# Chunked attention and a gated channel mix: scores in 64-row array tiles, softmax by units of 256 tokens, the gate in single PSUM banks

## The chip, the cores and the metric

The kernel runs on one core of a Trainium2 chip. The time is the device time of one execution in microseconds, as the median of several runs. The engines are named as in the profile: PE multiplies matrices (PEld is its weight loads), DVE works on vectors, ACT on scalar functions, POOL is the general engine, SP issues the transfers.

## What is computed

Four sequences of 768 tokens, 8 heads of 64. Attention is local: chunks of 32 queries see 16 tokens to the left, their own 32, 8 to the right, and 8 memory keys, 64 keys in all. The output, 512 wide, goes through a gated channel mix with a token shift.

```python
for c in range(S // 32):
    l_start, r_end = max(0, 32 * c - 16), min(S, 32 * c + 32 + 8)
    k_full = np.concatenate([mem_k, k[:, :, l_start:r_end]], axis=2)
    v_full = np.concatenate([mem_v, v[:, :, l_start:r_end]], axis=2)
    scores = scale * np.matmul(q_c, k_full.transpose(0, 1, 3, 2))
    a = np.exp(scores - scores.max(-1, keepdims=True))
    out[:, :, 32 * c : 32 * c + 32] = np.matmul(a / (a.sum(-1, keepdims=True) + 1e-9), v_full)
# x: out as (4, 768, 512)
xk = mu_k * x + (1 - mu_k) * x_prev          # x_prev: the token before
xr = mu_r * x + (1 - mu_r) * x_prev
k = np.maximum(xk @ w_k, 0)                  # 512 x 1024
v = k * k @ w_v                              # 1024 x 512
return 1 / (1 + np.exp(-(xr @ w_r))) * v     # 512 x 512
```

## The kernel before

Tokens come in query tiles of 128 (24 of them, four chunks of 32 each) and in units of 256, two tiles (12 units). Everything is float32. The three weight products of the channel mix are each done as three products of rounded parts (`fp32r`, high and low halves; `wkh` and `wkl` are the halves of `w_k`, `xh` and `xl` those of the mixed input).

For a tile, `attention` has these steps, named as the profile and the plan name them:

- **s**: 16 matmuls, one for each pair of heads and each chunk. The two heads of a pair lie in the two halves of the 128 rows. The host lays the queries out block-diagonally, with zeros for the other head, so that the 64 result columns are 32 queries of one head and 32 of the other. A matmul takes 128 rows and 64 columns, an even chunk writes partitions 0 to 63 and an odd one 64 to 127 of one PSUM bank (`s4[o : o + 64, ...]`).
- softmax on 512 columns: maximum (`mx`), subtraction (`e`), exponential, sum, normalisation on DVE or POOL.
- **t** (`pt`): four transposes; copies into `aTz`, whose other half is zero.
- **a** (`px`): 16 matmuls with `vw`, 64 columns each; a copy (`f_x`) turns the result into `xT`.

`prep` makes the mixed inputs of a unit (`df`, `xf`, then `xh` and `xl`, for the gate first). In `channel_mix`, **g** (`pr`) is the gate, 24 matmuls into a tile of two PSUM banks, which one sigmoid reads; **h** (`ph`) is the product with `w_k`, four groups of 24; **v** (`pv`) the product with `w_v`, 24 for each tile of the unit, planned in halves.

The order is set by a planner inside the kernel. `te_order` writes out a sequence for PE, beginning with `LEAD`, and derives due times from it with `PE_COST`; every step has an engine or a choice, a cost, and buffers (`Slot`, counted in `bufs`). `Plan.order` places steps greedily, and the result is issued in that order on every engine. Where the plan leaves PE idle before the first `ph`, the kernel issues matmuls on zeros (`warm`), their number worked out from the planned gap:

```python
n = 0 if ("ph", 0, 0) in T else int((o.start - busy - 0.2) / (0.22 if busy else 0.43))
```

[...] The buffers `big` hold query and key tiles (`qk`) and raw weights in turn.

Of the kernel before, what the change touches and what calls it, by code (L numbers as in the profile page):

```python
# [16 lines left out]
P = 128  # L17
# [23 lines left out]
PE_COST = {"s": 1.05, "t": 0.45, "a": 1.05, "g": BLOCK, "h": BLOCK, "v": BLOCK}  # L41
# [94 lines left out]
def te_order():  # L136

    nu = B * S // UTOK
    seq = LEAD.split()
    seq = [tuple([x[0]] + [int(n) for n in x[1:].split(".")]) for x in seq]  # L140
    for u in range(nu):
        a, b = 2 * u + 4, 2 * u + 5
        g = [("g", u + 1, c) for c in range(QPU)] if u + 1 < nu else []
        h = [("h", u, f) for f in range(FT // 2)]
        v = [("v", u, c, n) for c in range(QPU) for n in range(2)]
        seq += h[:2] + [("t", a)] + h[2:3] + [("a", a), ("s", b)] + h[3:] + g + [("t", b)]
        seq += v[:1] + [("a", b), ("s", a + 2)] + v[1:]
    nq = B * NQT
    seq = [x for x in seq if not (x[0] in "sta" and x[1] >= nq)]
# [9 lines left out]
def local_attention__then__channel_mix(  # L159
# [126 lines left out]
    xslot = {}  # L286

    def attention(t):
        b, i = qts[t]
        u, c = t // QPU, t % QPU  # L290

        def f_load():
            a = T["qk", t] = sb("big", [P, QKW], f"qk{t}")
            nc.sync.dma_start(a, qk[b, i])
# [5 lines left out]
        def f_s():  # L300
            s = T["s", t] = ps("s", f"s{t}")
            s4 = s.rearrange("p (m r k) -> p m r k", m=2, r=NPAIR)
            a = T["qk", t]
            nq = NPAIR * NJ * 2 * CHUNK
            q4 = a[:, :nq].rearrange("p (r j q) -> p r j q", r=NPAIR, j=NJ)
            k4 = a[:, nq:].rearrange("p (r j k) -> p r j k", r=NPAIR, j=NJ)
            for r in range(NPAIR):
                for j in range(NJ):
                    o = 64 * (j % 2)
                    nc.tensor.matmul(  # L310
                        s4[o : o + 64, j // 2, r, :], q4[:, r, j, :], k4[:, r, j, :], start=True, stop=True
                    )

        def f_max():
            s = T["s", t].rearrange("p (m r k) -> p m r k", m=2, r=NPAIR)
            if i == 0:
                nc.vector.memset(s[0:64, 0, :, 0:LEFT], NEG)
            if i == NQT - 1:
                nc.vector.memset(s[64:P, 1, :, LEFT + CHUNK : LEFT + CHUNK + RIGHT], NEG)
            mx = T["mx", t] = sb("sm", [P, 2 * NPAIR], f"mx{t}")  # L320
            nc.vector.reduce_max(mx, T["s", t].rearrange("p (g k) -> p g k", k=NK), axis=AX.X)  # L321

        def f_sub():
            e = T["e", t] = sb("e", [P, 2 * NPAIR, NK], f"e{t}")
            nc.vector.tensor_sub(  # L325
                e,
                T["s", t].rearrange("p (g k) -> p g k", k=NK),
                T["mx", t].unsqueeze(2).to_broadcast([P, 2 * NPAIR, NK]),
            )

        def f_exp():
            e = T["e", t]
            nc.scalar.activation(e, e, AF.Exp, scale=SCALE)  # L333

        def f_sum():
            sm = T["sum", t] = sb("sm", [P, 2 * NPAIR], f"sum{t}")
            nc.vector.reduce_sum(sm, T["e", t], axis=AX.X)
            nc.vector.tensor_scalar_add(sm, sm, 1e-9)
            nc.vector.reciprocal(sm, sm)  # L339

        def f_norm(g):
            e = T["e", t]
            g.tensor_mul(e, e, T["sum", t].unsqueeze(2).to_broadcast([P, 2 * NPAIR, NK]))  # L343
# [14 lines left out]
        def f_a():  # L358
            a = aTz[t % bufs["aT"]].rearrange("p (m g c h) s q -> p m g c h (s q)", m=2, g=2, c=2)
# [3 lines left out]
            for m in range(2):  # L363
                for cc in range(2):
                    for g in range(2):
                        for h in range(2):
                            j = 2 * m + cc
                            nc.tensor.matmul(  # L368
                                p3[64 * h : 64 * h + 64, 2 * g : 2 * g + 2, CHUNK * j : CHUNK * j + CHUNK],
                                v[:, g, h, j, :],  # L370
                                a[:, m, g, cc, h, :],
                                start=True,
                                stop=True,
                            )
# [13 lines left out]

        qs, vs, s1, s2, s3 = Slot("big"), Slot("vw"), Slot("s"), Slot("tp"), Slot("tp")
        m1, m2, e = Slot("sm"), Slot("sm"), Slot("e")  # L390
# [6 lines left out]
        o_s = op(("pe", 1.05), f_s, [l, prior.get("s")], new=[s1], use=[qs], due=ds)
        o_m = op(("dve", 0.62), f_max, [o_s], new=[m1], use=[s1], due=ds + 3)
        o_b = op(("dve", 0.62), f_sub, [o_m], new=[e], use=[s1, m1], due=ds + 4)
        o_e = op(("act", 0.55), f_exp, [o_b], use=[e])  # L400
        o_u = op(("dve", 0.98), f_sum, [o_e], new=[m2], use=[e])
        o_n = op(either(dve=(0.62, True), pool=(1.0, True)), f_norm, [o_u], use=[e, m2])
# [4 lines left out]
        prior.update(s=o_s, t=o_t, a=o_a)  # L407
# [3 lines left out]
        xdone[t] = op(either(act=(0.5,), dve=(0.61,)), f_x, deps, new=[xslot[u]] if c == 0 else [], use=[s3, xslot[u]], due=da + 4)  # L411
# [38 lines left out]
    def channel_mix(u):  # L450
        b, t0 = units[u]

        def f_gate(c):
            if c == 0:
                T["pr", u] = ps("g", f"pr{u}", QPU)
            p = T["pr", u][:, c * DM : (c + 1) * DM]
            xh, xl = T["xh", u, 1], T["xl", u, 1]
            wh, wl = ([w[k // 2][:, k % 2 * DM : (k % 2 + 1) * DM] for k in range(KT)] for w in wr_hl)
            for k in range(KT):
                for n, (x, w) in enumerate(((xh, wh[k]), (xh, wl[k]), (xl, wh[k]))):  # L460
                    nc.tensor.matmul(  # L461
                        p, x[:, k, c * P : (c + 1) * P], w, start=(k + n == 0), stop=(k == KT - 1 and n == 2)
                    )
# [13 lines left out]
        def f_sig():
            g = T["sg", u] = sb("sg", [P, QPU * DM], f"sg{u}")
            nc.scalar.activation(g, T["pr", u], AF.Sigmoid)

        sgs = Slot("sg")
        o_g = op(("act", 0.48 * QPU + 2.6), f_sig, grp, new=[sgs], use=[gs], due=due["g", u, 1] + BLOCK + 4)
# [49 lines left out]
        for c in range(QPU):  # L532
# [36 lines left out]
            o_o = op(("dve", 0.62), f_o, [prev, o_g], new=[os], use=[s, sgs], due=dv + BLOCK + 2)  # L569
# [4 lines left out]
    for t in range(len(qts)):  # L574
        attention(t)
# [67 lines left out]
```

## Time and profile before

| | |
|---|---|
| median of 3 runs | 439.28 us (439.17 to 439.79) |
| profiled execution | 439.1 us, its span 437.3 us |
| granted PE clock | 1.0 |
| busy: PE, DVE, ACT, POOL | 430.8, 257.8, 194.2, 26.4 us |
| `ph`, `pv`, `pr` in the chain that ended last | 30%, 30%, 15% of the span |
| `px`, `warm`, `s`, `pt` in it | 6%, 6%, 5%, 2% |

In the rows, `L310 PE MATMUL s<-qk 128*64 128x64 f32 x768` is line 310 of the kernel, the engine, the operation, output and inputs, rows times columns of the array, the shape, and how many records; then busy time, the mean time of one in ns, and the idle time of the engine before it with what ended it. In a timeline a row begins with its start and length in us. A matmul on float32 leaves two records, a transpose or one on rounded parts one.

### The profile page before, as it was taken

What the parts mean: (1) busy time and instruction counts of PE and PEld (TensorE: products, weight loads), DVE (VectorE), ACT (ScalarE), POOL (GpSimd) and SP (SyncE); (2) the same over time, 40 slices, a digit from 0 to 9 for tenths busy, and PEclk for the clock granted to TensorE, in tenths of its full rate; (3) what the DMA queues carried; (4) which work ended last, traced back from release to release, by engine and by line L of the source; (5) the groups of instructions that cost most, each with busy time, mean ns of one, the idle gap of its engine ahead of it and who ended that gap; (6) DMA issues with size and microseconds to landing.
All of it is one profiled execution on the core that took longest, in us unless ns stands there. A gap on an engine that the chain in (4) does not pass through costs nothing.

```text
span 437.3 us, 8807 instructions
## 1 busy us (share of the span) xinstructions
PE 430.8 (99%) x3868; PEld 382.6 (88%) x3868; DVE 257.8 (59%) x426; ACT 194.2 (44%) x266; POOL 26.4 (6%) x33
## 2 busy tenths in 40 slices
PE   9999999989999999999999999999999999999996
PEld 8899988888898898898898898898898898798894
DVE  2899999973654745744844835835736737522121
ACT  1767595552353353264254354354354354152150
POOL 2100030100100100100100100100100010000000
PEclk9999999999999999999999999999999999999999
DMA  8988767621331431421512422413401200000101
GB/s 323 411 318 298 295 247 272 257 93 51 143 130 45 165 105 53 183 68 79 190 54 94 171 69 100 169 43 128 168 28 46 73 25 1 25 25 0 49 0 48
DMA packets 12901, 55.15 MB, mean 126 GB/s; under 512 B 1472, under 2 KB 1600, under 8 KB 9280
## 3 DMA queue, kind: packets, MB, share of 16 engines
q1 hardware_dynamic: 12864, 54.60, 33.8%
q8 instruction: 30, 0.49, 0.5%
q14 instruction: 7, 0.06, 0.0%
HBM read 48.30 MB, written 6.29 MB: 125 GB/s over the span
## 4 chain that ended last, share of the span: by engine, by line
PE 94%; DVE 3%; ACT 2%; issue 0%
PE ph L493 30%; PE pv L549 30%; PE pr L461 15%; PE px L368 6%; PE warm L589 6%; PE s L310 5%; PE pt L349 2%; ACT aTz L215 1%; DVE e L343 1%; DVE o L563 0%; DVE df L432 0%; DVE mx L321 0%; ACT L333 0%; DVE xl L442 0%; DVE mag L264 0%; DVE df L424 0%
## 5 line engine op out<-in xcount | busy, mean ns | idle before, releaser
L493 PE MATMUL ph<-xh,wkh 128*128 128x256 f32 x384 | 109.6, 285 | 0.0
L493 PE MATMUL ph<-xh,wkl 128*128 128x256 f32 x384 | 107.8, 281 | 0.0
L493 PE MATMUL ph<-xl,wkh 128*128 128x256 f32 x384 | 107.8, 281 | 0.0
L549 PE MATMUL pv<-wvh,kh 128*128 128x512 f32 x192 | 77.8, 405 | 0.0
L549 PE MATMUL pv<-wvh,kl 128*128 128x512 f32 x192 | 76.1, 396 | 0.0
L549 PE MATMUL pv<-wvl,kh 128*128 128x512 f32 x192 | 75.6, 394 | 0.0
L493 PEld LDWEIGHTS ph<-xh,wkh 128*128 128x128 f32 x384 | 72.3, 188 | 1.2
L493 PEld LDWEIGHTS ph<-xl,wkh 128*128 128x128 f32 x384 | 72.4, 188 | 0.5
L493 PEld LDWEIGHTS ph<-xh,wkl 128*128 128x128 f32 x384 | 72.4, 188 | 0.0
L518 DVE TENSOR_TENSOR kl<-kf,kh 128x512 fp32r<-128x512 f32 x45 | 31.1, 691 | 69.7 <-ACT kh L215 69.6
L501 ACT ACTIVATE kf<-ph 128x512 f32<-128x512 f32 x48 | 28.7, 598 | 80.5 <-PE ph L493 80.5
L549 PEld LDWEIGHTS pv<-wvh,kl 128*128 128x128 f32 x192 | 36.0, 188 | 8.7
L549 PEld LDWEIGHTS pv<-wvh,kh 128*128 128x128 f32 x192 | 36.1, 188 | 8.4
L549 PEld LDWEIGHTS pv<-wvl,kh 128*128 128x128 f32 x192 | 36.1, 188 | 7.9
L461 PE MATMUL pr<-wrh,xl 128*128 128x512 f32 x96 | 38.1, 397 | 0.0
L461 PE MATMUL pr<-wrh,xh 128*128 128x512 f32 x96 | 38.0, 396 | 0.0
L461 PE MATMUL pr<-wrl,xh 128*128 128x512 f32 x96 | 37.8, 394 | 0.0
L217 DVE COPY aTz<-pt 64x512 f32<-64x512 f32 x29 | 20.0, 690 | 26.4 <-PE pt L349 26.3
L343 POOL TENSOR_TENSOR e<-e,sum 128x512 f32<-128x512 f32 x10 | 16.7, 1667 | 261.0 <-DVE sum L339 261.0
L424 DVE TENSOR_TENSOR df<-xT 128x1024 f32<-128x1024 f32 x12 | 14.7, 1223 | 28.7 <-ACT xT L215 28.7
L333 ACT ACTIVATE e<-e 128x512 f32<-128x512 f32 x24 | 15.2, 632 | 36.3 <-DVE e L325 36.2
L508 ACT ACTIVATE kf<-kf 128x512 f32<-128x512 f32 x48 | 30.3, 631 | 1.2
(55 smaller groups left out, 576.2 us busy)
## 6 DMA issues: line engine op xcount, KB each, us to landing
qk<-in_qk_dram SPq DMA_DIRECT2D x24, 1024.0 KB, 7.4
vw<-in_vw_dram SPq DMA_DIRECT2D x24, 512.0 KB, 3.8
out_dram<-o SPq DMA_DIRECT2D x24, 256.0 KB, 2.0
raw<-in_w_k_dram SPq DMA_DIRECT2D x4, 1024.0 KB, 5.3
raw<-in_w_v_dram SPq DMA_DIRECT2D x4, 1024.0 KB, 8.0
raw<-in_w_r_dram SPq DMA_DIRECT2D x2, 1024.0 KB, 9.8
id_sb<-in_ident_dram SPq DMA_DIRECT2D x1, 64.0 KB, 8.9
mu_sb<-in_mu_dram SPq DMA_DIRECT2D x1, 4.0 KB, 9.4
```

The source lines that it names most:

```text
L217: e.tensor_copy(dst, src)
L310: nc.tensor.matmul(s4[o : o + 64, j // 2, r, :], q4[:, r, j, :], k4[:, r, j, :], start=True, stop=True)
L333: nc.scalar.activation(e, e, AF.Exp, scale=SCALE)
L343: g.tensor_mul(e, e, T["sum", t].unsqueeze(2).to_broadcast([P, 2 * NPAIR, NK]))
L368: nc.tensor.matmul(p3[64 * h : 64 * h + 64, 2 * g : 2 * g + 2, CHUNK * j : CHUNK * j + CHUNK], v[:, g, h, j, :], a[:, m, g, cc, h, :], sta ...
L461: nc.tensor.matmul(p, x[:, k, c * P : (c + 1) * P], w, start=(k + n == 0), stop=(k == KT - 1 and n == 2))
L493: nc.tensor.matmul(p[:, i * UTOK : (i + 1) * UTOK], w[:, fc], x[:, k], start=(k + n == 0), stop=(k == KT - 1 and n == 2),)
L501: e.activation(r, T["ph", u, f], AF.Relu)
L508: e.activation(q, q, AF.Square)
L518: e.tensor_sub(l, T["kf", u, f], T["kh", u, f].bitcast(F32))
L549: nc.tensor.matmul(p, x[:, tc_], w, start=(f + n == 0), stop=(f == FT - 1 and n == 2))
L589: nc.tensor.matmul(warm[:, :P], zero_sb, zero_sb, start=True, stop=True)
```

## The change

- The scores are made for a unit: `scores(u)` takes both tiles. A matmul now has one head and one chunk: 64 rows (the half in which the head lies) by 32 columns (its 32 queries), written to the chunk's 32 partitions. The two heads of a pair go to two different PSUM banks; 64 matmuls per unit. The queries come without zeros, so that a `qk` tile has 1536 columns and not 2048.
- One softmax runs over the 1024 columns of both tiles. It can be normalised on DVE or POOL as before.
- The gate writes single `m` banks and has a sigmoid for each; the tag `g` is gone, `s` has two banks, `m` four.
- `big` has 4 buffers and not 3, `x4` 4 and not 5, `xT` 2 and not 3, `e` 1 (of double width) and not 2.
- The first column of `xT` is copied by ACT and not by POOL.
- PE's sequence is another: both px of a unit and the scores of the next but one stand together, and a unit's gate follows its px in the same pass.

```diff
-LEAD = "s0 t0 a0 s1 t1 a1 s2 t2 a2 s3 g0.0 g0.1 t3 a3 s4"
+LEAD = "s0 t0 t1 a0 a1 s1 g0.0 g0.1"
...
-QKW = NPAIR * NJ * (2 * CHUNK + NK)
+QKW = NPAIR * NJ * (CHUNK + NK)
...
-PE_COST = {"s": 1.05, "t": 0.45, "a": 1.05, "g": BLOCK, "h": BLOCK, "v": BLOCK}
+PE_COST = {"s": 1.9, "t": 0.45, "a": 1.05, "g": BLOCK, "h": BLOCK, "v": BLOCK}
...
-        a, b = 2 * u + 4, 2 * u + 5
-        g = [("g", u + 1, c) for c in range(QPU)] if u + 1 < nu else []
+        a, b = 2 * u + 2, 2 * u + 3
+        g = [("g", u + 1, c) for c in range(QPU)]
...
-        seq += h[:2] + [("t", a)] + h[2:3] + [("a", a), ("s", b)] + h[3:] + g + [("t", b)]
-        seq += v[:1] + [("a", b), ("s", a + 2)] + v[1:]
+        seq += h[:2] + [("t", a), ("t", b)] + h[2:3] + [("a", a), ("a", b), ("s", u + 2)] + h[3:]
+        seq += v[:1] + g + v[1:]
...
-        "big": 3, "vw": 2, "x4": 5,
-        "e": 2, "sm": 2, "xT": 3, "kf": 2, "sg": 2, "o": 3,
-        "s": 1, "tp": 2, "g": 1, "m": 3, "aT": 2,
+        "big": 4, "vw": 2, "x4": 4,
+        "e": 1, "sm": 2, "xT": 2, "kf": 2, "sg": 2, "o": 3,
+        "s": 1, "tp": 2, "m": 4, "aT": 2,
...
+    def scores(u):
...
+        def f_s():
+            s = T["s", u] = ps("s", f"s{u}", QPU)
+            s5 = s.rearrange("p (h c r k) -> p h c r k", h=2, c=QPU, r=NPAIR)
...
+            for c, t in enumerate(ts):
...
+                for r in range(NPAIR):
+                    for j in range(NJ):
+                        for h in range(2):
+                            z = slice(64 * h, 64 * h + 64)
+                            nc.tensor.matmul(
+                                s5[CHUNK * j : CHUNK * (j + 1), h, c, r, :], q4[z, r, j, :], k4[z, r, j, :],
+                                start=True, stop=True,
+                            )
...
+            nc.vector.reduce_max(mx, T["s", u].rearrange("p (g k) -> p g k", k=NK), axis=AX.X)
...
-            for r in range(NPAIR):
-                for j in range(NJ):
-                    o = 64 * (j % 2)
-                    nc.tensor.matmul(
-                        s4[o : o + 64, j // 2, r, :], q4[:, r, j, :], k4[:, r, j, :], start=True, stop=True
-                    )
...
-                    nc.gpsimd.tensor_copy(x[:, :, 0:1], T["xT", u - 1][:, :, UTOK : UTOK + 1])
+                    nc.scalar.copy(x[:, :, 0:1], T["xT", u - 1][:, :, UTOK : UTOK + 1])
...
-            if c == 0:
-                T["pr", u] = ps("g", f"pr{u}", QPU)
-            p = T["pr", u][:, c * DM : (c + 1) * DM]
+            p = T["pr", u, c] = ps("m", f"pr{u}_{c}")
...
+        def f_sig(c):
+            if c == 0:
+                T["sg", u] = sb("sg", [P, QPU * DM], f"sg{u}")
+            nc.scalar.activation(T["sg", u][:, c * DM : (c + 1) * DM], T["pr", u, c], AF.Sigmoid)
...
-    qbd = np.zeros((B, NQT, 2, D, NPAIR, NJ, 2, CHUNK), q.dtype)
-    for h in range(2):
-        qbd[:, :, h, :, :, :, h, :] = q7[:, :, h].transpose(0, 2, 5, 1, 3, 4)
-    qbd = qbd.reshape(B, NQT, P, -1)
+    qt = q7.transpose(0, 3, 2, 6, 1, 4, 5).reshape(B, NQT, P, -1)
```

Three places show what this does to the queues. First PE at the start of the program, before the first gate matmul; a row gives line, operation, output and inputs (with the number of the buffer) and how many. Before:

```order
L589 MATMUL warm<-zero_sb 128x128 x13
L310 MATMUL s_114<-qk_96 64x64 x16
L589 MATMUL warm<-zero_sb 128x128 x7
L310 MATMUL s_146<-qk_98 64x64 x16
L589 MATMUL warm<-zero_sb 128x128 x7
L310 MATMUL s_185<-qk_131 64x64 x16
L349 MATMUL pt_206<-id_sb,e_136 128x128 x4
L589 MATMUL warm<-zero_sb 128x128 x5
L368 MATMUL px_225<-aTz_86,vw_168 64x2x32 x16
```

And after, to the gate:

```order
L609 MATMUL warm<-zero_sb 128x128 x16
L311 MATMUL s_122<-qk_96 32x64 x32
L311 MATMUL s_122<-qk_98 32x64 x32
L609 MATMUL warm<-zero_sb 128x128 x32
L373 MATMUL pt_243<-id_sb,e_192 128x128 x4
L373 MATMUL pt_250<-id_sb,e_192 128x128 x4
L609 MATMUL warm<-zero_sb 128x128 x4
L390 MATMUL px_264<-aTz_86,vw_101 64x2x32 x16
L390 MATMUL px_285<-aTz_87,vw_103 64x2x32 x16
L609 MATMUL warm<-zero_sb 128x128
L311 MATMUL s_308<-qk_204 32x64 x32
L311 MATMUL s_308<-qk_248 32x64 x32
```

Three narrow scores with fillers between them have become one of both tiles, and the long filler stands behind it. Up to the first `ph` there are 110 fillers before and 123 after.

Second, PE in the steady part, where px and s stand between the matmuls of `ph`. Before (a second such pair stands inside `pv`):

```order
L493 MATMUL ph_2_1372<-xl_0_1161,wkh_69 128x256
L493 MATMUL ph_2_1372<-xh_0_1156,wkl_73 128x256
L368 MATMUL px_1404<-aTz_86,vw_1139 64x2x32 x16
L310 MATMUL s_1424<-qk_966 64x64 x16
L493 MATMUL ph_3_1450<-xh_0_1156,wkh_66 128x256
```

After, the only one of its unit:

```order
L511 MATMUL ph_2_1384<-xh_0_1243,wkl_73 128x256
L390 MATMUL px_1416<-aTz_86,vw_1090 64x2x32 x16
L390 MATMUL px_1436<-aTz_87,vw_1160 64x2x32 x16
L311 MATMUL s_1462<-qk_845 32x64 x32
L311 MATMUL s_1462<-qk_867 32x64 x32
L511 MATMUL ph_3_1532<-xh_0_1243,wkh_66 128x256
```

Both px of a unit and all its scores have moved into one place; behind it follow 24 `ph`, 24 `pv` and then the gate of the same unit.

Third, DVE in the steady part, from the copy of px to the low half of the gate's input (`xl_1`). Before:

```order
L217 COPY aTz_87<-pt_1523 64x16x32 x2
L424 TENSOR_TENSOR df_1582<-xT_1443 128x1024
L321 TENSOR_REDUCE mx_1598<-s_1562 128x8
L432 SCALAR_TENSOR_TENSOR xf_1600<-df_1582,mu_sb,xT_1443 128x256 x4
L325 TENSOR_TENSOR e_1618<-s_1562,mx_1598 128x512
L563 TENSOR_TENSOR o_0_1622<-pv_0_1530,sg_1184 128x512
L432 SCALAR_TENSOR_TENSOR df_1582<-df_1582,mu_sb,xT_1443 128x256 x4
```

After:

```order
L217 COPY xT_2558<-px_2519 128x4x128
L536 TENSOR_TENSOR kl_2_2563<-kf_2_2536,kh_2_2556 128x512
L438 TENSOR_TENSOR df_2633<-xT_2558 128x1024
L324 TENSOR_REDUCE mx_2660<-s_2565 128x16
L446 SCALAR_TENSOR_TENSOR xf_2664<-df_2633,mu_sb,xT_2558 128x256 x4
L328 TENSOR_TENSOR e_2686<-s_2565,mx_2660 128x1024
L446 SCALAR_TENSOR_TENSOR df_2633<-df_2633,mu_sb,xT_2558 128x256 x4
L456 TENSOR_TENSOR xl_1_2711<-xf_2664,xh_1_2688 128x1024
```

The steps from `df` to `xl_1` now follow the copy of the same unit's px, with the wide maximum and subtraction of the next scores among them.

More of the change, by code (lines that the diff above doesn't have):

```diff
@@ L141, in te_order @@
     for u in range(nu):
-        a, b = 2 * u + 4, 2 * u + 5
-        g = [("g", u + 1, c) for c in range(QPU)] if u + 1 < nu else []
+        a, b = 2 * u + 2, 2 * u + 3
+        g = [("g", u + 1, c) for c in range(QPU)]
         h = [("h", u, f) for f in range(FT // 2)]
         v = [("v", u, c, n) for c in range(QPU) for n in range(2)]
-        seq += h[:2] + [("t", a)] + h[2:3] + [("a", a), ("s", b)] + h[3:] + g + [("t", b)]
-        seq += v[:1] + [("a", b), ("s", a + 2)] + v[1:]
-    nq = B * NQT
-    seq = [x for x in seq if not (x[0] in "sta" and x[1] >= nq)]
+        seq += h[:2] + [("t", a), ("t", b)] + h[2:3] + [("a", a), ("a", b), ("s", u + 2)] + h[3:]
+        seq += v[:1] + g + v[1:]
+    last = {"s": nu, "g": nu, "t": B * NQT, "a": B * NQT}
+    seq = [x for x in seq if x[1] < last.get(x[0], nu)]
     due, t = {}, 8.0
@@ L331, in f_exp @@
[L331 to L343, printed above, removed]
         def f_t():
@@ L358, in f_a @@
         def f_a():
-            a = aTz[t % bufs["aT"]].rearrange("p (m g c h) s q -> p m g c h (s q)", m=2, g=2, c=2)
+            a = aTz[t % bufs["aT"]].rearrange("p (h g j) s q -> p h g j (s q)", h=2, g=2)
             v = T["vw", t].rearrange("p (g h j d) -> p g h j d", g=2, h=2, j=NJ)
@@ L362, in f_a @@
             p3 = p.rearrange("p (r q) -> p r q", r=NPAIR)
-            for m in range(2):
-                for cc in range(2):
-                    for g in range(2):
-                        for h in range(2):
[L367 to L374, printed above, removed]
+            for j in range(NJ):
+                for g in range(2):
+                    for h in range(2):
+                        nc.tensor.matmul(
+                            p3[64 * h : 64 * h + 64, 2 * g : 2 * g + 2, CHUNK * j : CHUNK * j + CHUNK],
+                            v[:, g, h, j, :],
+                            a[:, h, g, j, :],
+                            start=True,
+                            stop=True,
+                        )
         def f_x(e):
@@ L387, in f_x @@
             )
[L389 to L390 removed]
+        vs, s2, s3 = Slot("vw"), Slot("tp"), Slot("tp")
         az = Slot("aT")
@@ L393, in attention @@
             xslot[u] = Slot("xT")
-        ds, dt, da = (due[x, t] for x in "sta")
-        l = op(("dma", 3.0), f_load, new=[qs])
+        dt, da = due["t", t], due["a", t]
         lv = op(("dma", 1.5), f_loadv, new=[vs])
[L397 to L402, printed above, removed]
         o_t = op(("pe", 0.45), f_t, [o_n, o_id, prior.get("t")], new=[s2], use=[e], due=dt)
@@ L410, in attention @@
             deps.append(xdone[t - 1])
-        xdone[t] = op(either(act=(0.5,), dve=(0.61,)), f_x, deps, new=[xslot[u]] if c == 0 else [], use=[s3, xslot[u]], due=da + 4)
+        xdone[t] = op(either(act=(0.5,), dve=(0.61,)), f_x, deps, new=[xslot[u]] if c == 0 else [], use=[s3, xslot[u]], due=da + 3)
         if c == 0 and u > 0 and units[u][1] > 0:
@@ L463, in f_gate @@
                     )
-        gs = Slot("g")
+        def f_sig(c):
+            if c == 0:
+                T["sg", u] = sb("sg", [P, QPU * DM], f"sg{u}")
+            nc.scalar.activation(T["sg", u][:, c * DM : (c + 1) * DM], T["pr", u, c], AF.Sigmoid)
+        sgs = Slot("sg")
+        gs = [Slot("m") for _ in range(QPU)]
         grp = []
@@ L471, in channel_mix @@
                     grp[-1:] + list(mix[u, 1][:2]) + wdeps(wr_hl, range(KT // 2)),
-                    new=[gs] if c == 0 else [], use=list(mix[u, 1][2:]) + ([gs] if c else []),
-                    due=due["g", u, c],
-                )
-            )
[L477 to L482, printed above, removed]
+                    new=[gs[c]], use=list(mix[u, 1][2:]), due=due["g", u, c],
+                )
+            )
+        o_g = []
+        for c in range(QPU):
+            o_g.append(
+                op(
+                    ("act", 0.5 + 1.3 * (c == 0)), lambda c=c: f_sig(c), grp[c : c + 1] + o_g[-1:],
+                    new=[sgs] if c == 0 else [], use=[gs[c], sgs], due=due["g", u, QPU - 1] + BLOCK + 2,
+                )
+            )
         ks = []
@@ L568, in channel_mix @@
             os = Slot("o")
-            o_o = op(("dve", 0.62), f_o, [prev, o_g], new=[os], use=[s, sgs], due=dv + BLOCK + 2)
+            o_o = op(("dve", 0.62), f_o, [prev, o_g[c]], new=[os], use=[s, sgs], due=dv + BLOCK + 2)
             op(("dma", 0.75), f_st, [o_o], use=[os], due=dv + BLOCK + 6)
@@ L573, in local_attention__then__channel_mix @@
         weight(i)
-    for t in range(len(qts)):
-        attention(t)
+    for u in range(NU):
+        soft = scores(u)
+        for t in range(u * QPU, (u + 1) * QPU):
+            attention(t, *soft)
     for u in range(NU):
@@ L613 @@
     q7 = q.reshape(B, NPAIR, 2, NQT, NJ, CHUNK, D)
-    qbd = np.zeros((B, NQT, 2, D, NPAIR, NJ, 2, CHUNK), q.dtype)
-    for h in range(2):
-        qbd[:, :, h, :, :, :, h, :] = q7[:, :, h].transpose(0, 2, 5, 1, 3, 4)
-    qbd = qbd.reshape(B, NQT, P, -1)
+    qt = q7.transpose(0, 3, 2, 6, 1, 4, 5).reshape(B, NQT, P, -1)
     kw = windows(k, mem_k).reshape(B, NPAIR, 2, NQT, NJ, NK, D)
@@ L622 @@
     arrays = {
-        "qk": np.concatenate([qbd, kw], axis=3),
+        "qk": np.concatenate([qt, kw], axis=3),
         "vw": vw,
```

81 lines of the change are left out of this document (52 added, 29 removed).

## The prediction

> **What bounds the kernel now.** I read the page first: busy times, slices and the chain that ended last.
>
> ```profile
> PE 430.8 (99%) x3868; PEld 382.6 (88%) x3868; DVE 257.8 (59%) x426; ACT 194.2 (44%) x266; POOL 26.4 (6%) x33
> DVE  2899999973654745744844835835736737522121
> PE 94%; DVE 3%; ACT 2%; issue 0%
> ```
>
> PE is busy for 99% of the span and carries 94% of the chain. DVE is full only in slices 3 to 8, about 22 to 87 us. So there are two questions: what PE has to do once the real work runs, and when that starts. The busy times by stage separate them (window, its length, then PE, PEld, DVE, ACT and POOL busy with their instructions, the granted clock, DMA share, GB/s):
>
> ```profile
> 0.00:47.02 47.02, 45.50 (x548) 42.30 (x549) 36.93 (x57) 26.87 (x31) 4.60 (x12) 1.00 0.88 334
> 82.50:115.90 33.40, 32.30 (x261) 27.86 (x260) 23.44 (x39) 12.72 (x18) 2.62 (x3) 1.00 0.31 117
> 149.40:182.90 33.50, 33.50 (x307) 29.64 (x306) 19.35 (x36) 14.37 (x20) 1.81 (x3) 1.00 0.31 111
> 433.50:437.30 3.80, 0.00 (x0) 0.00 (x0) 0.68 (x1) 0.00 (x0) 0.00 (x0) 1.00 0.18 69
> ```
>
> The first `ph` matmul is issued at 47.02. From there to 433.5 PE has work in every microsecond but one, in the second unit (32.30 of 33.40 us). A unit of 256 tokens takes 33.5 us, of which DVE works 19 and the DMA engines a third. There only PE's own time counts. The start-up of 47.02 us is another matter: PE mostly runs `warm` fillers, and DVE prepares weights.
>
> ```profile
> 17.69 0.69 DVE L260 TENSOR_SCALAR raw<-raw 128x1024 uint32<-128x1024 uint32 x1
> 43.33 3.48 DVE L270 TENSOR_TENSOR wkl<-mag,wkh 128x1024 fp32r<-128x1024 f32 x3
> ```
>
> From its first weight step at 17.69 to the last half of `w_k` at 46.81 (43.33 + 3.48) DVE hardly pauses, and 0.2 us later PE begins `ph`. DVE sets the start.
>
> **Scores on PE: the term that decides.** Twice per unit a px and an s stand together between ordinary matmuls:
>
> ```profile
> 171.92 0.40 PE L549 MATMUL pv<-wvh,kl 128*128 128x512 f32 x1
> 172.24 1.15 PE L368 MATMUL px<-aTz,vw 128*64 128x64 f32 x32
> 173.22 1.10 PE L310 MATMUL s<-qk 128*64 128x64 f32 x32
> 174.26 0.50 PE L549 MATMUL pv<-wvh,kh 128*128 128x512 f32 x1
> 174.59 0.40 PE L549 MATMUL pv<-wvl,kh 128*128 128x512 f32 x1
> 174.83 0.40 PE L549 MATMUL pv<-wvh,kl 128*128 128x512 f32 x1
> ```
>
> From 171.92 to 174.59 two pv steps pass, of about 0.235 (174.59 to 174.83), so the block costs 2.67 - 0.47 = 2.20 us. Each matmul leaves two records (32 for 16). The s row is 1.10 long and its last record 0.222 (next fence), so 31 steps take 0.88 us, 0.028 each. For what one record takes alone, compare fillers on the whole array:
>
> ```profile
> L310 PE MATMUL s<-qk x768: 222/222/271, 5.9 to 361.0; 128*64 128x64 f32 x192
> 19.56 5.18 PE L589 MATMUL warm<-zero_sb 128*128 128x128 f32 x44
> L589 PE MATMUL warm<-zero_sb x220: 274/275/582, 1.1 to 47.0; 128*128 128x128 f32 x110
> ```
>
> (5.18 - 0.275) / 43 is 0.114 us for 128 streamed columns, so 64 columns take about 0.057, and s runs at half that: two array tiles of 64 columns work at a time. How they share the array shows where an s had not been queued ahead; the timeline, cut off ever later, there gives:
>
> ```profile
> 8.83 0.24 PE L310 MATMUL s<-qk 128*64 128x64 f32 x1
> 8.83 0.28 PE L310 MATMUL s<-qk 128*64 128x64 f32 x2
> 8.83 0.30 PE L310 MATMUL s<-qk 128*64 128x64 f32 x3
> 8.83 0.34 PE L310 MATMUL s<-qk 128*64 128x64 f32 x4
> 8.83 0.36 PE L310 MATMUL s<-qk 128*64 128x64 f32 x5
> 8.83 0.39 PE L310 MATMUL s<-qk 128*64 128x64 f32 x6
> ```
>
> The ends lie 0.04, 0.02, 0.04, 0.02, 0.03 apart: records 1, 3, 5 are one series with a step of 0.06, records 2, 4, 6 another, out of step with it. I read them as two tiles that each keep their own pace of 0.058 us. One queue for both would not let the second series begin inside the first one's record. Without its records' time the block leaves 2.20 - 64 x 0.029 = 0.34 us for going from the full array to tiles and back.
>
> Now the change. A unit has 64 score matmuls of 64 rows by 32 columns where it had 32: 128 records, each still of 64 streamed columns, 0.058 on its tile. They rotate over 4 column groups and 2 row halves. With n tiles at work the scores of a unit take S = 128 x 0.058 / n: 0.93 us for 8, 1.86 for 4, 3.71 for 2; before, 64 records on two tiles took 1.86. Nothing in this trace runs more than 2 at once, so the bounds are 0.93 and 3.71. I take 1.0 (eight, and 0.07 until the last has begun), since the six rows show tiles that do not wait for one another. Whether the feed keeps up is open too: in these blocks PE takes 64 instructions in 0.93 us (a weight load per record) and would have to take 256.
>
> [...]
>
> The sum from the first `ph` on needs the counts of tiles that remain (640 records of px, 608 of s), and the blocks, 22 in the chain, from first to last:
>
> ```profile
> 47.02:433.47 386.45, 23.04 (x640) 20.28 (x640) 1.00 0.28 101
> 47.02:433.47 386.45, 21.06 (x608) 19.36 (x608) 1.00 0.28 101
> 56.16 1.08 PE s L310 x32
> 373.11 1.08 PE px L368 x32
> ```
>
> Before: 20 tiles of px and 19 of s at 0.93 are 36.3 us, 22 blocks at 0.34 are 7.5: 43.8. After: px of 21 tiles 19.5, one block for each of 11 units 3.7, ten changes from 64-column to 32-column tiles inside them 1.5 (0.15 each, between nothing and the 0.34 of a whole round trip), and 10 S: 24.7 + 10 S. The difference is 10 S - 19.1: **-9.1 us** at S = 1.0, between -9.8 at 0.93 and +18.0 at 3.71.
>
> **Start-up.** The first softmax now waits for 2 x 768 KB, where the first had 1024 KB and the second twice that. They began at 5.9 and 8.83 (rows above); I put the joint scores at 7.2, between them, and their end at 8.2. For the softmax the rows are one of double width on DVE and one on ACT, and a small one:
>
> ```profile
> L424 DVE TENSOR_TENSOR df<-xT 128x1024 f32<-128x1024 f32 x12 | 14.7, 1223 | 28.7 <-ACT xT L215 28.7
> L257 ACT ACTIVATE mag<-raw 128x1024 f32<-128x1024 f32 x10 | 11.6, 1164 | 1.0 <-DMA raw<-in_w_v_dram 1.0
> L339 DVE RECIPROCAL sum<-sum 128x8 f32<-128x8 f32 x24 | 4.9, 203 | 0.8
> L325 DVE TENSOR_TENSOR e<-s,mx 128x512 f32<-128x512 f32 x24 | 16.5, 686 | 0.5
> ```
>
> Maximum, subtraction and sum at 1.22, exp 1.16, two small ones of 0.2 come to 5.2, with handovers 5.5: at 13.7 DVE turns to weights, 4.0 earlier than 17.69, since one softmax and not three stands ahead. From there to the last `wkl` it took 29.1 us. The new order keeps all weight and mixing steps, drops two `aTz` copies (1.2) and a narrow softmax (2.9: four at 0.6, the distance of their starts, and the small ones), and puts in a wide softmax and a wide normalisation (6.1): 31.1, so 44.8. PE has 123 fillers for 110, at two records of 0.112 each 2.9 us more, and a px and an s tile fewer; from 7.2 its own list adds up to about 46. I put the first `ph` at **46.3, -0.7 us**, between 44.8 and 48.
>
> **Smaller parts.** The gate in two banks costs ACT two sigmoids for one, some 0.2 more; ACT has 19 of 33.5 us free, so 0. Ten normalisations go from POOL to DVE, 1.2 each; DVE has 14 us free per unit, 0. Smaller loads at a DMA share of 0.31: 0. Eight groups per unit now share four `m` banks; between a bank's last matmul and its next use lies at least one `ph` group, so 0.
>
> One wait gets tight. The gate of a unit now follows its px within the same unit, where before `xT` was ready a unit ahead.
>
> ```profile
> L215 ACT COPY xT<-px 128x512 f32<-128x512 f32 x14 | 8.2, 587 | 31.3 <-PE px L368 31.2
> L432 DVE SCALAR_TENSOR_TENSOR df<-df,mu_sb,xT 128x256 f32<-128x256 f32 x48 | 20.0, 477 | 0.0
> 155.59 2.81 PE ph L493 x24
> 169.51 2.80 PE pv L549 x12
> ```
>
> From the end of px: a copy 0.6 and its handovers 0.25, then in DVE's queue df 1.22, the maximum 1.22, xf 4 x 0.48, the subtraction 1.22, the other mixing 1.91, xl 1.22: 9.6 with whole durations, about 8.8 as starts overlap. PE meanwhile does S, the change back, one `ph` and two halves of `pv`: 1.0 + 0.3 + 2.81 + 5.6 = 9.7. So 0, but with a cover of under 1 us; beyond it every 0.1 us costs 1 us in ten units. Behind the waiting gate stand the second halves of `pv`, and behind these the output.
>
> The tail of 3.8 us stays. Sum: 437.3 - 0.7 - 9.1 = 427.5 of span. The profiled execution had 439.1, 1.8 outside its span, so 429.3, and the median of the runs lies 0.2 above that: **429.5**.
>
> **Rivals.**
> 1. Only the four column groups overlap, the row halves do not: S = 1.86, as long as before, and the change does not do what it says. For it: no row here has two row halves. PE -0.5, start-up -0.7 + 0.9 for the later softmax: 439.0.
> 2. Slower: PE looks only so far ahead in its queue that two tiles work at a time, or its feed binds. For it: two is all that the trace shows. Against: the series out of step. Two tiles: +18.0 on PE and +2.0 in the start-up, 459.3. Halfway, three tiles or S = 2.5: +5.9 and +0.8, 446.0. The point: 10 S - 19.1 - 0.7 + (S - 1.0) is nil at S = 1.89, 30 ns a matmul.
> 3. The gate waits 0.8 us in each unit for `xl`, since a copy or cast on the way is late: +8, 437.5. For it: a cover under 1 us; against: DVE idle for 14 us of a unit.
>
> **How the numbers follow.** Eight tiles (S up to 1.3) 0.50, with a range of its own from 427 to 434: the start-up 1.5 either way, S to 1.3. Rival 1 0.24, rival 2 0.18, rival 3 0.08. Within 0.2%, 438.4 to 440.2, is about what a measurement of this kernel can tell from no change. Rival 1 parts into 0.09 faster, 0.08 same and 0.07 slower; rival 3 gives 0.05, 0.02 and 0.01. Together: faster 0.64, same 0.10, slower 0.26. The range goes from the lower end of the first case over rivals 1 and 3 well into rival 2, to S = 3.2, between three tiles and two (+12.9 and +1.5, 453.7): 427 to 454.
>
> **What will show it.** The 128 s records of a unit within 1.3 us say eight tiles, 2.1 us four, near 4 two. A block of px and s of 3.3 us between two `ph` groups and a unit of 32.3 us say the sum holds. A wait of pr for xl says rival 3. A first `ph` later than 48, or PE idle for `wvl` between 55 and 75, would spoil the start-up term.

## The result and the profile after

The changed kernel takes 432.57 us (median, 431.57 to 433.23) where the kernel before took 439.53 beside it: a ratio of 0.9837, with an interval from 0.9811 to 0.9863. Forecast were 429.5 and a range from 427 to 454. The profiled execution has a span of 431.5.

The page of the changed kernel: busy times, and the chain by engine.

```profile
PE 417.0 (97%) x4662; PEld 375.3 (87%) x4662; DVE 245.2 (57%) x348; ACT 209.3 (48%) x294; POOL 4.4 (1%) x13
PE 87%; ACT 3%; DVE 3%; issue 3%; DMA 2%; SPq 1%; DVEq 0%; ACTq 0%
```

PE is busy for 2% less of the span, and the chain has 3% of "issue": time in which PE waited for nothing that the profile shows. Before it had 0%. The windows give the start-up, one unit and the tail (window, its length, PE, PEld, DVE, ACT and POOL busy, clock, DMA share, GB/s):

```profile
0.00:48.87 48.87, 43.78 (x638) 41.42 (x638) 36.34 (x46) 29.75 (x33) 2.38 (x9) 1.00 0.81 312
163.00:195.01 32.01, 32.01 (x369) 28.76 (x369) 18.14 (x28) 15.73 (x23) 0.10 (x1) 1.00 0.30 107
427.59:431.50 3.91, 0.00 (x0) 0.00 (x0) 0.69 (x1) 0.00 (x0) 0.00 (x0) 0.95 0.18 67
```

So `ph` starts 1.85 us later than before (47.02), PE's work from there lasts 378.72 us instead of 386.45, and the tail of 3.91 us is 0.1 longer. A unit without "issue" takes 32.0 us; 32.3 were forecast. The block of px and s, in the timeline of a unit and in the chain of waits (start, length):

```profile
156.56 2.08 PE L390 MATMUL px<-aTz,vw 128*64 128x64 f32 x64
158.58 1.48 PE L311 MATMUL s<-qk 64*32 64x64 f32 x128
159.99 0.38 PE L511 MATMUL ph<-xh,wkh 128*128 128x256 f32 x1
```

```profile
91.35 1.41 PE s L311 x89
92.76 0.56 PE ph L511 x3
93.32 1.36 issue
94.68 2.64 PE ph L511 x21
168.49 5.49 PE pr L473 x24
179.48 5.47 PE ph L511 x48
```

Where PE does not stop, all 128 records of a unit's scores start within 1.27 us: at 0.058 us a record that is 5.8 tiles at work on average, and all eight at first (the first 32 start within 0.24 us). But in six of the ten units with scores PE then stands still for 0.5 to 1.4 us, here after three `ph`, elsewhere inside s. The list of PE's waits adds them up (the third row is the start-up):

```profile
PE s L311 <- issue: 2.9, 4, 0.9
PE ph L511 <- issue: 2.6, 2, 1.4
PE px L390 <- issue: 1.1, 1, 1.1
```

That is 5.5 us which no step of the prediction had. (From the start of the last matmul to the start of the next, less a usual step, the six stops come to 6.6 us: the profile counts a pause only from the end of a matmul.) One more thing is new: `pr` takes 5.49 us for 24 matmuls and 48 of `ph` 5.47, where before it was

```profile
149.46 5.70 PE ph L493 x48
163.48 5.59 PE pr L461 x24
```

Over the run the mean step from one matmul to the next fell from 233.4 to 229.6 ns for `pv` and `pr`, and from 118.2 to 114.8 for `ph`.

### The profile page after: what moved, and what is told of

Its sections match the earlier page's. It is cut to its first block, busy times and chain, and to the rows that moved or that the text cites. A ratio compares the mean times of both kernels' runs of the same rounds, so it can differ in the third digit from the quotient of the medians.

```text
span 431.5 us, 10287 instructions
## 1 busy us (share of the span) xinstructions
PE 417.0 (97%) x4662; PEld 375.3 (87%) x4662; DVE 245.2 (57%) x348; ACT 209.3 (48%) x294; POOL 4.4 (1%) x13
## 4 chain that ended last, share of the span: by engine, by line
PE 87%; ACT 3%; DVE 3%; issue 3%; DMA 2%; SPq 1%; DVEq 0%; ACTq 0%
PE ph L511 31%; PE pv L567 31%; PE pr L473 14%; PE px L390 5%; PE s L311 3%; DMA raw<-in_w_r_dram 2%; PE pt L373 2%; ACT mag L257 1%; ACT wkh L215 1%; ACT L480 1%; DVE raw L260 1%; DVE xf L446 0%; ACT L336 0%; DVE df L446 0%; DVE mag L264 0%
## 5 line engine op out<-in xcount | busy, mean ns | idle before, releaser
L511 PE MATMUL ph<-xl,wkh 128*128 128x256 f32 x384 | 106.6, 278 | 0.0
L511 PE MATMUL ph<-xh,wkl 128*128 128x256 f32 x384 | 106.6, 278 | 0.0
L567 PE MATMUL pv<-wvh,kh 128*128 128x512 f32 x192 | 74.9, 390 | 0.0
L536 DVE TENSOR_TENSOR kl<-kf,kh 128x512 fp32r<-128x512 f32 x47 | 32.5, 691 | 56.7 <-ACT kh L215 56.5
L581 DVE TENSOR_TENSOR o<-pv,sg 128x512 f32<-128x512 f32 x24 | 16.6, 691 | 69.9 <-PE pv L567 69.9
L609 PE MATMUL warm<-zero_sb 128*128 128x128 f32 x246 | 30.6, 286 | 1.0 <-DVE zero_sb L204 1.0
L609 PEld LDWEIGHTS warm<-zero_sb 128*128 128x128 f32 x246 | 29.7, 201 | 1.4 <-DVE zero_sb L204 1.0
L480 ACT ACTIVATE sg<-pr 128x512 f32<-128x512 f32 x24 | 14.3, 597 | 34.1 <-PE pr L473 34.0
```

Of the source, the lines that this page charges most:

```text
L480: nc.scalar.activation(T["sg", u][:, c * DM : (c + 1) * DM], T["pr", u, c], AF.Sigmoid)
L511: nc.tensor.matmul(p[:, i * UTOK : (i + 1) * UTOK], w[:, fc], x[:, k], start=(k + n == 0), stop=(k == KT - 1 and n == 2),)
L536: e.tensor_sub(l, T["kf", u, f], T["kh", u, f].bitcast(F32))
L567: nc.tensor.matmul(p, x[:, tc_], w, start=(f + n == 0), stop=(f == FT - 1 and n == 2))
L581: nc.vector.tensor_mul(o, T["pv", u, c], T["sg", u][:, c * DM : (c + 1) * DM])
L609: nc.tensor.matmul(warm[:, :P], zero_sb, zero_sb, start=True, stop=True)
```

## The experiments

Each run is timed beside the kernel before, and ratios are to it. In the quoted expectations, "distance" is the place of a unit's first score in PE's own list of instructions, beyond the last multiple of 256. I count two instructions for a record (weight load and matmul), from the program's start. Why 256: the profile has a DMA queue for instructions, and the trace lists 36 transfers on it, each of 16384 bytes.

```profile
q8 instruction: 36, 0.59, 0.6%
```

36 pieces make 0.59 MB, and 4662 records make 9324 instructions, 259 to a piece; in the kernel before 30 pieces stand against 7736 instructions, 258. I take 256, as an estimate from these two. A unit has 736 instructions (192 + 96 + 48 for `ph`, `pv`, `pr`, 16 for `pt`, 128 for `px`, 256 for s), 32 short of three pieces, so the distance falls by 32 from unit to unit:

| unit | 3 | 4 | 5 | 6 | 7 | 8 | 9 | 10 | 11 | 12 |
|---|---|---|---|---|---|---|---|---|---|---|
| distance | 205 | 173 | 141 | 109 | 77 | 45 | 13 | 237 | 205 | 173 |
| pause, us | 0.70 | 1.36 | 1.24 | 0 | 0 | 0 | 0 | 0.47 | 0.80 | 0.93 |

The pauses seem to go with the distance, not with the time. That was the theory to test: px and s issue 384 instructions in 2.02 + 1.41 us (the expectation below says 2.3; 3.4 is right), and a piece that is needed inside comes too late.

### The distance held still

```diff
+EXTRA = 7
...
+            if u > 1:
+                for n in range(EXTRA):                 # writes the same scores again
+                    j, h = n // 2 % NJ, n % 2
+                    z = slice(64 * h, 64 * h + 64)
+                    nc.tensor.matmul(
+                        s5[CHUNK * j : CHUNK * (j + 1), h, c, 0, :], q4[z, 0, j, :], k4[z, 0, j, :],
+                        start=True, stop=True,
+                    )
```

> The changed kernel, with seven score matmuls of each unit from the third on issued a second time (same operands, same result). A unit then has 764 instructions in PE's queue instead of 736, so that the distance of the scores from the last multiple of 256 instructions stays where it is in the third unit (205 by my count), instead of moving on by 32 with each unit. Theory, instructions come late: PE fetches its instructions in pieces of 256 (16 KB), and px with s takes 384 of them in 2.3 us, while a piece takes over 2 us to come. Then a pause stands in every one of the ten units, 0.5 to 0.9 us, near the 100th to 120th of the s records: 5 to 9 us in all, where the changed kernel has 5.5 in six units. The repeats cost 14 records of 0.010, 0.14 a unit or 1.4. Time 433.5 to 437.5. Rival, the pauses hang on something in time (transfers, a semaphore): they stand in the same six units, about 5.5 in all, and the time is 434.0.

> As the run with the distance held at 205, but 33 of the fillers ahead of the first gate are 66 of half the width, which puts 132 instructions more ahead of the third unit: the distance stands at 81 in every unit, where the changed kernel had no pause. Theory, instructions come late: no pause in any unit, 432.6 - 5.5 + 1.4 = 428.5, and 5 to 9 us under the run with 205. Rival, something in time: pauses in the same six units, 434.0, as in the run with 205.

With the distance at 205: 440.28 us, ratio 1.0025 (1.0009 to 1.0040), slower than the kernel before. At 81: 433.35, ratio 0.9862 (0.9849 to 0.9874). PE's waits at 205:

```profile
PE s L312 <- issue: 9.6, 10, 2.0
```

In every unit with scores there is a pause now, at its longest 2.0. At 81 the same list has no "issue" at all. The rival (six units, equal times) is out: the place in the instruction list decides. (764 instructions are 4 short of three pieces, so the distance is not quite held: it falls by 4 a unit, from 205 to 169 and from 81 to 45.)

The traces also time every transfer on the instruction queue, and they bear the theory out. With PE's semaphore waits counted in, all sixteen pauses, the six of the changed kernel and the ten at 205, end at the same instruction of a piece (193 beyond a multiple of 256), and each ends 1.0 to 1.6 us after a transfer of 16 KB has landed. In thirteen of them the transfer began within 0.5 us of the moment when PE crossed the boundary before, and 2.2 to 2.9 us passed from that boundary to the next; PE was through with the 256 instructions sooner. At 94.68 the transfer began 0.2 us after the boundary, took 1.8 and landed so late that 3.4 us passed.

Three misses. At 205 the pauses were 0.4 to 2.0 and not 0.5 to 0.9. The time at 205 was 2.8 us above the range: the pauses add up to 9.6, and behind the longest one the granted clock was 0.50 (window, length, busy times, clock, DMA share, GB/s):

```profile
196.30:199.20 2.90, 2.90 (x16) 2.90 (x15) 2.90 (x6) 0.00 (x0) 0.00 (x0) 0.50 0.94 349
```

At 81 the time did not come to 428.5, because the narrow fillers put ahead of the gate are no faster than wide ones:

```profile
22.61 15.18 PE L618 MATMUL warm<-zero_sb 128*128 128x128 f32 x134
```

15.18 / 134 is 0.113 us a record, and 132 of the 134 are 64 columns wide (the row names the shape of the two others). The first `ph` came at 53.8 instead of 48.9, and from there the run took 431.0 - 53.8 = 377.2 us, where the changed kernel took 382.6. That is 5.4 less in spite of 1.6 for the repeats (the s block lasts 0.16 longer), 7.0 without them: about the 6.6 that the six pauses cost from start to start.

### The burst made smaller

```diff
...
-        seq += h[:2] + [("t", a), ("t", b)] + h[2:3] + [("a", a), ("a", b), ("s", u + 2)] + h[3:]
+        seq += h[:2] + [("t", a), ("t", b), ("s", u + 2, 0)] + h[2:3] + [("a", a), ("a", b), ("s", u + 2, 1)] + h[3:]
...
```

> The changed kernel with the later sigmoids and the scores of a unit in two steps of 64 records: the first tile's behind pt, the second tile's behind px, one group of ph apart. No repeats, the distance from the multiples of 256 moves as in the changed kernel. Theory: what starves PE is 256 instructions in under about 2.4 us, so px with half of the scores (256 in 2.0 + 0.65 and a change of tiles) is at the edge, and pauses are gone or under 0.4 us whatever the distance; a unit costs one more change to tiles and back, 0.3, and the second ramp of a score block, 0.1: -5.5 + 4, about 429.5 with the start-up at 46.3. Rival: a pause needs no burst, only a multiple of 256 inside a tile block: pauses of 0.5 to 1.4 in five to seven of ten units stay, 433 or more.

427.47 us, ratio 0.9709 (0.9690 to 0.9729), with the later sigmoids described below. Here the distance moves on, and still PE has no "issue" from the first `ph` (44.08) to the end; px waits twice for copies on ACT in the first unit, 1.5 us. A later unit:

```profile
158.31:190.59 32.28, 32.28 (x370) 28.78 (x369) 17.97 (x28) 15.88 (x23) 0.11 (x1) 1.00 0.28 98
```

32.28 is 0.27 above an undisturbed unit of the changed kernel. From the first `ph` on the run takes 381.5 us, 1.1 less than the changed kernel; the other 4.8 that its span is shorter lie in the start-up, where the second unit's px now stands behind two groups of `ph`. Several boundaries of a piece fall inside a tile block here, so that does no harm by itself. What starves PE is 256 instructions that it gets through sooner than the next piece comes: with the scores in two, never fewer than 3.3 us lie between one boundary and the next from the first `ph` on. The two runs with the distance, the transfers and this run together show that the pauses are late instructions.

### How many tiles work at once

The loops of the scores in another order: heads outermost (four column groups in turn), or chunks outermost (two row halves in turn).

```diff
-                for r in range(NPAIR):
-                    for j in range(NJ):
-                        for h in range(2):
+                for h in range(2):                 # four;  two: for j, for r, for h
+                    for r in range(NPAIR):
+                        for j in range(NJ):
```

> The changed kernel with the loop over the two heads of a pair outermost: a run of matmuls turns over the four column groups of one row half, then over those of the other. [...] Time 434 to 438.5. Rival, the feed alone sets 1.27 and the order of tiles does not matter: 432.6.

> The changed kernel with the loop over chunks outermost and over the heads of a pair innermost: a run of eight matmuls alternates between the two row halves of one column group. Theory, tiles work independently and in the order of issue: two at a time, S = 3.71, 2.44 more in ten units, +24; the pauses of 5.5 go, since 384 instructions then take over 4 us. Time 451 to 457. Rival, tiles of the same columns and different rows do not work at once: S = 7.4, 488. Second rival, the feed alone sets the pace: 432.6.

Four: 435.47, ratio 0.9911 (0.9898 to 0.9924). Two: 439.06, ratio 0.9993 (0.9982 to 1.0003), as slow as the kernel before. The s block in a unit, four and two:

```profile
191.88 1.73 PE L311 MATMUL s<-qk 64*32 64x64 f32 x128
```

```profile
193.03 2.46 PE L311 MATMUL s<-qk 64*32 64x64 f32 x128
```

Less the last record's 0.22, S is 1.52 and 2.24, against 1.27: the order of tiles matters, and the feed alone would have left all three alike. Both are shorter than 128 x 0.058 / n (1.86 and 3.71), so my size for them was wrong. The 434 to 438.5 for four was this 1.86, 0.6 more than 1.27 in each of ten units, +6, less 0 to 5 for shorter pauses. PE stops less as the block lasts longer: 4.8 us in s and `ph` with four and 0.9 with two, where the changed kernel has 5.5. In the second run eight matmuls in a row use the same two tiles. Its records begin in pairs, at first 56 ns from pair to pair, as tiles at 0.058 us a record would have it; eight such groups one behind the other would take 3.6 us. But from the eleventh record on other pairs start among them, and a group takes 0.28 us and not 0.45. The trace does not name a record's tile; I read it as PE taking up the next group while a tile is busy. At eight tiles the first 32 records start within 0.24 us, 7.5 ns apart, the other 96 take 1.03, 10.7 each; eight tiles of 0.058 would give 7.3. I read the difference as the feed, two instructions in 10.7 ns; no run tests it.

### Which part brought the gain

```diff
-                            s5[CHUNK * j : CHUNK * (j + 1), h, c, r, :], q4[z, r, j, :], k4[z, r, j, :],
+                        s4[o : o + 64, c, j // 2, r, :], q4[:, r, j, :], k4[:, r, j, :],   # queries with zeros, 128 rows
```

> The changed kernel with the scores done as before (128 rows, 64 columns, block-diagonal queries with zeros, loads of 1024 KB); order, joint softmax and gate stay as changed. The question is what the order alone is worth and whose the shorter steps are. The scores of a unit last 1.86 us as in the kernel before, +5.9; a unit issues 608 instructions and px with s 256 in 3.9 us, so no pauses, -5.5; the scores of the first unit wait for larger loads, +1. Theory, the shorter steps (0.229 for 0.233, 0.113 for 0.118) come with the order: 434. Rival, they come with the tiles of 64 rows: another +5 to +6, 439 to 440, as long as the kernel before.

> The kernel before with one part of the change alone: the gate in single PSUM banks of the pool that ph and pv use (four banks for three and the pair), with a sigmoid for each. Theory, this part is worth nothing: 439.4, between 438.6 and 440.2, and the matmuls keep their steps of 0.231 to 0.234 (pr, pv) and 0.117 to 0.119 (ph). Rival, the banks or the order that comes with them are what gave the changed kernel its shorter steps of 0.229 and 0.113: 434 to 436.

The scores on 128 rows in the new order: 434.58, ratio 0.9890 (0.9876 to 0.9904). So order, joint softmax and gate bring about 4.9 of the 7.0 us, and the tiles of 64 rows as they stand 2.0. PE in this run has no pause, and its chain shows what the tiles gain and lose:

```profile
158.12 1.87 PE s L310 x64
168.53 5.49 PE pr L473 x24
179.51 5.66 PE ph L511 x48
```

s takes 1.87 for 1.41, so ten units would give 4.6, and the pauses take that back and more. What is left lies in the start-up (the first `ph` at 50.02 here, where the loads are larger too) and in the steps. `pr` has its 5.49 here too, so the 229 ns come with the new order, and theory was right on that half; `ph` stays at 5.66, so its shorter steps come with the 64-row tiles, as the rival said. The gate alone: 438.81, ratio 0.9986 (0.9977 to 0.9996), steps as before:

```profile
149.56 5.70 PE ph L497 x48
163.58 5.59 PE pr L459 x24
```

So the banks are not the cause. What order and joint softmax bring each was not separated, and why the order of the program shortens a step by 4 ns is open.

### The start-up

```diff
-        ready = [(d.end, d.eng) for d in o.deps]
+        ready = [(d.end, d.eng) for d in o.deps + o.hold]
...
+        if t == 2 * QPU - 1:
+            T["c3"] = c1                       # the last aTz copy of the second unit
...
+        hold = [T["c3"]] if u == 0 else []
...
+            o_g[-1].hold = hold
```

In the changed kernel ACT stood from 34.41 to 40.58 at two sigmoids, an exponential and three table loads, and DVE and PE waited for ACT just before the first `ph`:

```profile
34.41 1.28 ACT L480 ACT_TABLE_LOAD   x1
35.70 0.60 ACT L480 ACTIVATE sg<-pr 128x512 f32<-128x512 f32 x1
36.32 1.28 ACT L336 ACT_TABLE_LOAD   x1
37.61 1.06 ACT L336 ACTIVATE e<-e 128x1024 f32<-128x1024 f32 x1
38.69 1.28 ACT L480 ACT_TABLE_LOAD   x1
39.98 0.60 ACT L480 ACTIVATE sg<-pr 128x512 f32<-128x512 f32 x1
```

```profile
41.65 2.36 DVE L264 SCALAR_TENSOR_TENSOR mag<-mag,raw 128x1024 uint32<-128x1024 uint32 x2 [1.23 <-ACT mag L257]
46.70 1.23 DVE L270 TENSOR_TENSOR wkl<-mag,wkh 128x1024 fp32r<-128x1024 f32 x1 [0.42 <-ACT wkh L215]
47.79 1.15 PE L390 MATMUL px<-aTz,vw 128*64 128x64 f32 x32 [0.76 <-ACT aTz L215]
```

> The changed kernel, with the two sigmoids of the first gate held back on ACT until the copies into aTz for the second unit are done. On ACT they and their three table loads stood from 34.41 to 40.58, ahead of the last three mag and two wkh. Theory, ACT's queue set the start-up: the exponential then needs no table and ends near 36.3, the mag that DVE waited for come 1.2 earlier, the last wkl ends near 46.2 and the first ph starts near 47.4 instead of 48.9: 431.1, 1.5 under the changed kernel. The pauses stay as they are, since PE's list keeps its numbers. Rival, DVE's own list sets the start-up: the first ph stays at 48.9, 432.6.

The last `wkl` now ends at 45.43 and the first `ph` starts at 46.28, 2.6 earlier. The time did not follow: 432.83, ratio 0.9837 (0.9807 to 0.9868). From the first `ph` on the run took 385.6 us for 382.6: the pauses came to 6.3 us for 5.5, the longest of them grew to 2.0, and PE ran slowly after it.

```profile
93.31 0.28 PE L516 MATMUL ph<-xh,wkh 128*128 128x256 f32 x1 [2.02 <-issue]
95.09 0.41 PE L516 MATMUL ph<-xl,wkh 128*128 128x256 f32 x1
```

The same stretch by windows (length, PE busy, clock, DMA share, GB/s):

```profile
91.30:93.31 2.01, 0.00 (x0) 1.00 1.04 256
93.31:94.45 1.14, 1.14 (x10) 1.00 0.83 318
94.45:97.60 3.15, 3.15 (x15) 0.51 0.91 378
```

So ACT did set the start-up, which confirms the theory. The gain went into longer pauses, which the theory had taken as constant, and into 3 us at half clock. The long pause lies where the DMA engines are full: SP had just issued the loads of `vw` and `qk` (88.43 to 91.09). The piece's transfer began 1.5 us after PE had crossed the boundary before. Over all runs 32 pauses of 0.3 us and more end at a boundary. In eleven the DMA engines were over 60% busy from the boundary before until the piece had landed, and in ten of these its transfer began 0.9 to 3.4 us late; in 19 of the other 21 it began less than 0.7 late. That full DMA engines make the piece late is therefore likely; no run changes them alone.

### Both together

> The repeats that hold the distance of the scores at 81, but with 38 fillers on tiles of 64 rows and 32 columns in place of five whole ones ahead of the first gate, instead of the narrow ones that took 5 us; and the first sigmoids held back as in the run with the sigmoids later. Theory, the two effects are separate: no pauses (-5.5), repeats +1.4, start-up -1.5: 427.0. Rival, the pauses were not lost time but cover for something else that is late (the gate for xl, whose cover is 1.06): waits of pr appear and half of the gain is gone, 429.8.

> As the run that joins the steady 81 and the later sigmoids, and in the start-up the transposes of the second unit are held back behind the first group of ph (the sigmoids stand behind the last wkh). Theory, after ACT the chain over the second unit's softmax, pt and aTz is what the first ph stands behind: without it ph starts when the last wkl is done, near 46.2, 1.2 earlier than in the run without this, 425.8. Rival, the time comes back as a wait of px or of the gate of the second unit, since its softmax is no earlier: 427.0.

> The steady distance and the later sigmoids together, as in the run that had 38 small fillers and lost 5 us by them ahead of the first gate. Here the distance is set without a burst: of each long row of fillers two thirds become half as many of double width, 128 instructions fewer in the same time, which puts the scores at 77. Theory: first ph at 46.3 as in the run with the sigmoids later, and from there 377.2 us as in the run at 81 (431.0 - 53.8), span 423.5, time 425.3; no pause. Rival, the time gained at the start comes back as a wait for wvl or for the gate's xl in the second unit: 427 or more, with that wait in PE's list.

> As the run with wide fillers, but the narrowing of PE's list is done behind the second unit's scores alone (the rows of fillers around the first gate, half as many of double width), so that these scores stand at 101 as in the changed kernel and not at 61, where PE stopped for 2.4 us inside them and then ran its fillers at half pace. The scores from the third unit on stand at 73. Theory: no pause anywhere, first ph at 46.3, and 377.2 from there: span 423.5, time 425.3. Rival: in the start-up, where the transfers take 80% and more of the DMA engines, a piece of instructions is late wherever it falls, PE stops elsewhere for 1 to 3 us and the first ph comes at 48 or later: 427 to 429.

The first three got 431.75, 430.57 and 428.52 (ratios 0.9820, 0.9790, 0.9753), all slower than expected and mainly for one reason: in the start-up, too, a burst starved PE. In the first two it was the block of small fillers (2.6 us of "issue"), in the third the second unit's scores at a distance of 61:

```profile
21.93 2.39 issue
24.32 1.19 PE s L313 x65
25.50 8.49 PE warm L625 x46
```

The granted clock fell to 0.5 at 23.82, inside the pause, and stayed there until 27.23; over the first 4.5 us of the fillers it was 0.81 (next row: window, length, busy times, clock, DMA share, GB/s), and `ph` came at 49.5.

```profile
25.50:30.00 4.50, 4.50 (x18) 3.86 (x18) 4.46 (x9) 1.62 (x2) 0.00 (x0) 0.81 0.94 346
```

The second run thus says nothing on pt behind `ph`. With these scores left at 101 it went as forecast:

```diff
+                k = n // 2 if n >= 33 else 0        # long rows of fillers: half as many, twice as wide
```

425.92 us, ratio 0.9692 (0.9678 to 0.9707), first `ph` at 46.42, and PE's waits have no "issue":

```profile
PE warm L625 <- DVE zero_sb L206: 1.2, 1, 1.2
PE pt L383 <- DVE e L356: 0.5, 1, 0.5
PE pr L485 <- DVE xl L468: 0.2, 1, 0.2
PE px L400 <- ACT aTz L217: 0.2, 1, 0.2
```

This version beats both kernels. The one with the scores in two steps lies close (0.9709, overlapping intervals) and needs no counting of instructions.

## Why the prediction was right, and where its steps were not

The time lay in the range and on the right side, and the likeliest case (eight tiles) was the real one. But the sum of 427.5 us of span was 4.0 short of 431.5, and that it was no further off is luck: two terms that it did not have nearly cancel.

- **Eight tiles, S = 1.0.** Right in kind: 1.27 us, inside the 1.3 that the prediction set for eight. The size was off by 0.27, or +2.7 us in ten units: after some 32 records the steps lengthen, as I read it by the feed. "Whether the feed keeps up is open" was the right doubt, but it took the feed as a steady pace and left out that it comes in pieces.
- **The upper end of the range.** It was carried to S = 3.2. No run shows that term: in its place the runs showed 1.27 with eight tiles, 1.52 with four in turn and 2.24 with two, and the changed kernel's 128 records start 7 to 11 ns apart on average.
- **The change from px to s at 0.15.** It is the difference of px to s between the runs with 64-row and with 128-row scores, 0.152 - 0.052 = 0.10: -0.5 in ten units.
- **Missing: pauses for instructions.** +5.5 us by the profile, +6.6 from start to start. The prediction counted 256 instructions for 64 but looked only at PE's pace, not at where they come from.
- **Missing: shorter steps.** 1152 `ph` at 3.4 ns and 864 `pv` and `pr` at 3.8 ns less are -3.9 and -3.3, together -7.2. No row of before spoke for it.
- **From the first `ph` on** these make -9.1 + 2.7 - 0.5 + 6.6 - 7.2 = -7.5; measured -7.7.
- **Start-up, -0.7.** Wrong: +1.85, beyond the 48 named as the sign of it. DVE turned to the weights at 13.72, as forecast (13.7). The step that failed is the stretch of 31.1: it summed DVE's work and took ACT as free. From 13.72 to the end of the last `wkl` at 47.93 it took 34.2. On ACT stood two sigmoids with three table loads, and the run with the later sigmoids brought the first `ph` forward by 2.6.
- **Smaller parts at 0.** The gate alone moved the time by -0.14%, so it was nearly right; in the start-up, though, its two sigmoids on ACT were not free: an exponential between them made three table loads.
- **The gate's cover under 1 us.** Right: in an undisturbed unit the last part of `xl` ends at 167.4 and pr starts at 168.5. Rival 3 did not happen; only in three of the runs with several changes did pr wait for `xl`, 0.2 to 0.5 us, once.
- **Rivals 1 and 2.** Neither four nor two tiles. The orders that put four or two in turn cost 435.47 and 439.06, less than the 439.0 and 459.3 of the rivals, since S was 1.52 and 2.24 and not 1.86 and 3.71.

## What to carry to other kernels

When a change multiplies the instructions of an engine, count them against the time in which they are consumed, not only per instruction: a dense block of small matmuls can be fast by itself and starve the next stretch. The sign in the profile is "issue" ahead of PE that comes and goes with the place in the program; split the burst, so that 256 instructions take longer than the next piece needs (here 3.3 us was enough, and a piece whose transfer began at the boundary before took 2.2 to 2.9, once 3.4). A start-up is the chain over all engines in order of issue, so an engine with half its time free can still stand in the way.

## What the hardware showed beyond that

- PE's instructions came in pieces of 16384 bytes over a DMA queue (36 in the changed kernel); when a burst outran them, PE stood for up to 2.6 us, until 1.0 to 1.6 us after the piece had landed.
- With pauses of 2.0 to 2.6 us PE's granted clock fell to 0.5 for 3.4 us (23.82 to 27.23 with wide fillers; once 6.8): 1.2 and 1.5 us after PE resumed from the two of 2.0 (sigmoids later, distance 205), during the longer ones or at their end. With waits of 1.36 and 1.79 us it did not.
- A filler of half the width took as long: 0.113 us a record in the row of 134 above, where the whole width took 0.114 in the kernel before ((5.18 - 0.275) / 43).
- Dense matmuls ran at two paces, 229 and 233 ns for 512 columns (5.49 and 5.59 us for 24 `pr`) and 114 and 118 for 256 (5.47 and 5.66 us for 48 `ph`). A group of matmuls between two pauses or small blocks mostly kept one of them; what sets it is open.
